# Pooled attention and a four-expert mixture: keys and values loaded as two accumulating halves, and weight combinations moved

## The chip, the cores and the metric

The kernel runs on one core of one Trainium2 chip. A core has five engines that run side by side, each through its own list of instructions in order: TensorE (PE, matrix products), VectorE (DVE), ScalarE (ACT), GpSimd (POOL) and SyncE (SP). POOL and SP here mostly start transfers (DMAs), which 16 DMA engines carry out. Engines wait for each other and for transfers through semaphores. The metric is the device time of one execution in microseconds (us); lower is better. The program before takes 526.44 us (median of three runs, 525.48 to 526.85). The profiled execution took 525.31 us, and its profile spans 523.6 us, at a granted TensorE clock of 0.998.

## The reference

Two computations follow each other. First, attention with pooled keys and values, for 8 batches, 8 heads, 576 positions and 64 columns: each group of eight consecutive positions of k and v is averaged to 72 positions, and every query attends to these.

```
k_p = k.reshape(B, H, 72, 8, D).mean(axis=3)      # v_p likewise
scores = q @ k_p^T / sqrt(D)
attn = exp(scores - max);  attn = attn / sum(attn)
x = attn @ v_p
```

Then a mixture of four experts on the 4608 rows of x (512 columns), with normalised probabilities p:

```
out = sum over e of  p[:, e] * ( relu(x @ w1[e]) @ w2[e] )     # w1: 512x1024, w2: 1024x512
```

## The kernel before, in words

**Order of the work.** The rows are taken in nine chunks c of 512: chunks 0 to 7 are the first 512 positions of each batch, chunk 8 collects the 64 remaining positions of all batches. For each chunk there are four steps, one per expert e. In a step, PE makes the expert's first product (the functions up_plain, up_half and up_seven, or up_down, which also makes the step before's second product), and down makes the second product of the step before. The attention of batch b = c + 1 is woven into chunk c, so that its x is ready when chunk b begins.

**Seven products instead of eight.** up_seven and up_down multiply 2x2 blocks with seven block products instead of eight. This needs sums and differences of blocks: of the weights w1 (combine_w1(e), four operations of 128x1024 each, L586 to L589), of w2 for experts 1 and 2 (combine_w2, L626 to L629), of x (forms_of, L602) and of the hidden values (sums_of, L701 to L704). They run on DVE, except combine_w2 of expert 2 and combine_w1 of expert 0, which are given to POOL. Expert 0 uses plain products (up_half, up_plain) in chunks 0 and 1 and the seven products from chunk 2 on; expert 1 uses plain products in chunk 0 alone. S3 overwrites the block A21, so it may only be formed once the plain products with that block are done.

**How the order is written.** The order on each engine is written out by hand. The code counts points: each step has 16, reached by point() and slot(). A plan maps a point to small functions (the plans of second_attention and attention(c); in the latter the entry n stands for point 2n + 1 of the chunk, so n runs from 0 to 31). slot() also takes the next function from the list forms_due, which holds the combinations. An entry `lambda: None` in that list, called nothing, delays the rest by one slot. Such a position sets the order in which an engine gets its instructions, and which earlier ones it must wait for; an engine whose inputs are ready does not wait for PE to reach the point.

**Keys and values.** load_kv fetches one batch's k or v on POOL's queue as 72 partitions x 8 heads x 8 positions x 64 columns, turned from float32 to bf16 on the way. DVE then adds the eight positions in three halvings: first adds 4 to 4 (L205, 72x1024), rest adds 2 to 2 (L210, 72x512) and 1 to 1 into the pooled tile (L213; twice for keys, into kp, and once for values, into vps). All this is done for two halves of the heads. All k, and v of batches 3 to 7, use one buffer, raw; v of batches 1 and 2 use the space of w2_t, which later holds the combined w2. Because there is one buffer, the values of a batch can only be fetched when its keys are folded, and the next keys when the values are folded.

**Around it.** keys(b) transposes the pooled keys by a transfer of SP (kp to kpT, L227), queries(b) the queries (L245), turn the finished x (L406). loads_wait is a one-element copy on POOL that waits for kpT (L234), and so holds POOL's later loads back until that transpose has landed. scores (L262, exponent at L266), context (L385, then reciprocal and division on DVE, L366 and L367) are the attention proper. On DVE there are further the relu sums of the seven products (L686), which free the PSUM banks that PE writes next, and the additions into the output rows (L761, L831).

Of the kernel before, what the change touches and what calls it, by code (L numbers as in the profile page):

```python
# [11 lines left out]
ALU = mybir.AluOpType  # L12
AX = mybir.AxisListType
BF16 = mybir.dt.bfloat16
# [4 lines left out]
def kernel(  # L19
# [55 lines left out]
    w2_t = wpool.tile([P, len(SPLIT), 3, FCH // 2, TH], BF16, name="w2_t")  # L75
    h_s = wpool.tile([P, 3, FCH // 2, TH], BF16, name="h_s")

    raws = {}
    q_rems = {}

# [1 line left out]
    halves = [slice(i * H // 2, (i + 1) * H // 2) for i in range(2)]  # L82

    def load_kv(b, src, nm):
        if b in (1, 2) and nm == "vraw":
            raw = w2_t[0:SP].rearrange("p a b f d -> p (a b f d)")[:, 0:H * POOL * D].rearrange(
                "p (h r d) -> p h r d", h=H, r=POOL
            )
        else:
            raw = rawpool.tile([SP, H, POOL, D], BF16, name="raw")[:]  # L90
        nc.gpsimd.dma_start(
            out=raw, in_=src[b].rearrange("h (j r) d -> j h r d", r=POOL)
        )
        raws[(nm, b)] = raw

    def load_first(src, nm, hs):
        if nm not in raws:
# [34 lines left out]
    def load_k(b):  # L132
        load_kv(b, k, "kraw")

    def load_v(b):
        load_kv(b, v, "vraw")
# [64 lines left out]
    def fold_parts(nm, b, hs, last):  # L201

        def first():
            raw = raws[(nm, b)]
            nc.vector.tensor_add(out=raw[:, hs, 0:4, :], in0=raw[:, hs, 0:4, :],  # L205
                                 in1=raw[:, hs, 4:8, :])

        def rest():
            raw = raws[(nm, b)]
            nc.vector.tensor_add(out=raw[:, hs, 0:2, :], in0=raw[:, hs, 0:2, :],  # L210
                                 in1=raw[:, hs, 2:4, :])
            for out in last(hs):
                nc.vector.tensor_add(out=out, in0=raw[:, hs, 0, :], in1=raw[:, hs, 1, :])  # L213

        return [first, rest]

    def key_parts(b):
        return [part for hs in halves for part in fold_parts(
            "kraw", b, hs, lambda hs: [kp[0:SP, hs, dup, :] for dup in range(2)])]
# [13 lines left out]
    def loads_wait(b):  # L233
        nc.gpsimd.tensor_copy(out=mark[:], in_=state[("kpT", b)][0:1, 0, 0:1])  # L234
# [268 lines left out]
    def second_attention():  # L503

        lo, hi = halves

        return {
            42: [lambda: fold_keys(1, lo)],
            44: [lambda: fold_keys(1, hi), lambda: load_k(2)],
            47: [second_keys],  # L510
            50: [lambda: second_queries(0)],
            51: [lambda: second_queries(1), lambda: load_q(2), lambda: load_q_rem(2)],
            53: [lambda: scores(1, 0)],
            55: [lambda: scores(1, 1)],
            56: [lambda: fold_values(1, lo)],
            57: [lambda: scores(1, 2)],
            58: [lambda: fold_values(1, hi)],
            59: [lambda: scores(1, 3)],
            60: [lambda: context(1, 0), lambda: turn(1, 0)],
            61: [lambda: context(1, 1), lambda: turn(1, 1)],  # L520
            62: [lambda: context(1, 2), lambda: turn(1, 2)],
            63: [lambda: context(1, 3), lambda: turn(1, 3)],
            66: [lambda: load_v(2)],
        }

    def attention(c):

        lo, hi = halves
        b = c + 1
        plan = {}  # L530

        def add(n, *what):
            plan.setdefault(n, []).extend(what)

        if c % 2:
            i = c // 2
            add(18, lambda: rem_queries(i))
            add(23, lambda: rem_scores(i))
            add(26, lambda: rem_context(i))
            add(27, lambda: rem_turn(i))  # L540
        if b == B:
            for part in forms_of(B):
                add(31, part)
            return plan
        if c == 1:
            keyed = 1
            add(0, lambda: queries(b))
            for n, part in enumerate(key_parts(b)):
                add(n // 2, part)
        else:  # L550
            keyed = 1
            for n, part in enumerate(key_parts(b)[2:]):
                add(n, part)
        scored, valued, mixed = 7, 8 if c > 1 else 6, 11
        add(keyed, lambda: keys(b), lambda: loads_wait(b))
        if c > 1:
            add(keyed + 1, lambda: load_v(b))
        if b + 1 < B:
            add(keyed + 1, lambda: (load_q(b + 1), load_q_rem(b + 1)))
        for pair in range(NPAIR):  # L560
            add(scored + pair, lambda pair=pair: scores(b, pair))
        for n, part in enumerate(value_parts(b)):
            add(valued + n, part)
        if b + 1 < B:
            add(valued + 4, lambda: queries(b + 1), lambda: load_k(b + 1))
            for n, part in enumerate(key_parts(b + 1)[:2]):
                add(30 + n, part)
        for r in range(NR):
            add(mixed + r, lambda r=r: context(b, r))
            add(mixed + 1 + r, lambda r=r: turn(b, r))  # L570
        for n, part in enumerate(forms_of(b)):
            add((20, 21, 28, 29)[n], part)
        return plan
# [274 lines left out]
    with tc.manual_schedule(engines={ENG.PE, ENG.DVE, ENG.Activation, ENG.Pool, ENG.SP}):  # L848
# [52 lines left out]
        for s in range(len(steps) + 1):  # L901
# [84 lines left out]
```

The softmax here doesn't subtract the row's maximum and nothing guards it: scores larger than these inputs give would overflow.

## Time and profile before

| what | value |
|---|---|
| median time | 526.44 us |
| span of the profile | 523.6 us |
| PE busy | 504.0 us (96%) |
| DVE busy | 355.4 us (68%) |
| ACT busy | 267.5 us (51%) |
| POOL busy | 67.5 us (13%) |
| POOL's loads (queue q0) | 33744 packets, 31.0% of 16 DMA engines |
| k and v loads, whole batches | 14 of 576 KB each |

A busy row gives the time in which an engine had an instruction running, with its share of the span and the number of instructions. In the second part of the page the span is cut into 40 slices of 13.1 us, and a digit is the busy share in tenths. A line of the timeline gives start, duration, engine, line of the code, operation, output and inputs by tile name, shapes and number; the brackets at its end give the idle time before it and what ended that. In a table of stages the columns are the stretch, its length, then for PE, its weight loads, DVE, ACT and POOL the busy us and the number of instructions, the granted clock, the busy share of the DMA engines and their GB/s.

### The profile page before, as it was taken

How to read it: one execution, taken by the hardware profiler on the slowest of the kernel's cores; microseconds unless marked ns; L12 is line 12 of the kernel's file. 1: busy time of each engine (PE TensorE's matmuls, PEld its weight loads, DVE VectorE, ACT ScalarE, POOL GpSimd, SP SyncE). 2: the span in 40 equal slices, each digit the busy share in tenths (PEclk: the TensorE clock that was granted, in tenths of full speed). 3: DMA queues.
4: the chain of work that ended last, by engine and by line, in shares of the span. 5: the costliest groups of instructions: out<-in, count | busy, mean ns of one | idle time of the engine just before them, and what ended most of it. 6: DMA issues, size and time to landing. Idle time of an engine off the chain costs nothing.

```text
span 523.6 us, 10155 instructions
## 1 busy us (share of the span) xinstructions
PE 504.0 (96%) x4171; PEld 363.5 (69%) x4171; DVE 355.4 (68%) x649; ACT 267.5 (51%) x467; POOL 67.5 (13%) x80
## 2 busy tenths in 40 slices
PE   8898989969999999999999999999999999999996
PEld 4745644558757876688668866886588768866883
DVE  2434787897857884878677876787677546764674
ACT  3653434636465545565465546653655446544650
POOL 8362102860020002000100020000000000000000
PEclk9999999999999999999999999999999999999999
DMA  9999999510199207920696059403510110011003
GB/s 133 207 206 206 199 149 179 107 30 1 24 169 107 25 0 142 145 36 11 106 143 65 2 94 157 70 11 57 94 32 0 41 52 1 11 42 40 1 1 80
DMA packets 75133, 41.56 MB, mean 79 GB/s; under 512 B 44480, under 2 KB 70464, under 8 KB 75088
## 3 DMA queue, kind: packets, MB, share of 16 engines
q0 software_dynamic: 33744, 22.63, 31.0%
q1 hardware_dynamic: 41344, 18.29, 18.7%
q8 instruction: 32, 0.52, 0.4%
q14 instruction: 13, 0.11, 0.1%
HBM read 45.16 MB, written 9.44 MB: 104 GB/s over the span
## 4 chain that ended last, share of the span: by engine, by line
PE 71%; DVE 13%; DMA 10%; POOL 2%; issue 2%; ACT 1%; POOLq 0%; ACTq 0%; SPq 0%; DVEq 0%
PE g_ps L638 30%; PE o_ps L817 19%; PE u_ps L755 16%; DMA w_bf<-in_moe_w_dram 5%; DMA raw<-in_v_dram 3%; DVE H_sb L686 3%; DVE acc L761 3%; DMA kpT<-kp 2%; PE h_ps L656 1%; PE two L262 1%; PE two L385 1%; POOL w_bf L142 1%; DVE h_s L701 1%; DVE x_tok L367 1%; DVE H_sb L702 1%
## 5 line engine op out<-in xcount | busy, mean ns | idle before, releaser
L638 PEld LDWEIGHTS <-w_bf 128*128 128x128 bf16 x1848 | 176.1, 98 | 49.5 <-issue 10.7
L817 PE MATMUL o_ps<-w_bf,H_sb 128*128 128x512 bf16 x640 | 161.5, 379 | 0.2 <-DMA w_bf<-in_moe_w_dram 0.2
L682 ACT COPY r<-g_ps 128x512 f32<-128x512 f32 x166 | 97.4, 586 | 106.3 <-PE g_ps L638 102.4
L638 PE MATMUL g_ps<-xf,w_bf 128*128 128x256 bf16 x1056 | 148.4, 272 | 2.8 <-DVE H_sb L686 1.8
L686 DVE CUSTOM_DVE_ANT_0 H_sb<-g_ps,r 128x512 bf16<-128x512 f32 x166 | 113.9, 687 | 48.1 <-ACT r L682 33.3
L761 DVE SCALAR_TENSOR_TENSOR acc<-u_ps,p_all,acc 128x512 f32<-128x512 f32 (+1 forms) x128 | 78.0, 612 | 43.8 <-ACT u_ps L781 43.1
L638 PE MATMUL g_ps<-xT,w_bf 128*128 128x256 bf16 x696 | 99.9, 273 | 2.0 <-DVE H_sb L686 2.0
L817 PEld LDWEIGHTS <-H_sb 128*128 128x128 bf16 x640 | 62.5, 98 | 46.1 <-issue 0.4
L689 ACT ACTIVATE H_sb<-g_ps 128x512 bf16<-128x512 f32 x98 | 58.4, 596 | 29.7 <-PE g_ps L638 29.7
L755 PEld LDWEIGHTS <-H_sb 128*128 128x128 bf16 x512 | 49.4, 98 | 8.2 <-DVE H_sb L702 2.4
L755 PE MATMUL u_ps<-w_bf,H_sb 128*128 128x256 bf16 x384 | 52.4, 273 | 1.1 <-DVE H_sb L702 0.9
L755 PEld LDWEIGHTS <-h_s 128*128 128x128 bf16 x384 | 37.5, 98 | 6.1 <-DVE h_s L703 1.8
L831 DVE SCALAR_TENSOR_TENSOR acc<-o_ps,p_all,acc 128x512 f32<-128x512 f32 x44 | 32.7, 746 | 11.3 <-PE o_ps L817 11.3
L755 PE MATMUL u_ps<-w_t,h_s 128*128 128x256 bf16 x256 | 38.4, 273 | 1.5 <-DVE h_s L703 1.5
L266 ACT ACTIVATE expT<-two 72x1024 bf16<-72x1024 f32 x28 | 28.6, 1020 | 13.4 <-PE two L262 13.4
L767 ACT COPY g_ps<-g_ps 128x512 f32<-128x512 f32 x32 | 18.3, 572 | 27.9 <-PE g_ps L638 27.9
L828 ACT ACTIVATE acc<-o_ps,p_all 128x512 f32<-128x512 f32 x36 | 24.8, 690 | 7.0 <-PE o_ps L817 7.0
L234 POOL COPY mark<-kpT 1x1 bf16<-1x1 bf16 x6 | 1.3, 218 | 205.9 <-DMA kpT<-kp 205.9
L781 ACT COPY u_ps<-u_ps 128x256 f32<-128x256 f32 x32 | 11.4, 357 | 26.7 <-PE u_ps L755 26.7
L205 DVE TENSOR_TENSOR raw<-raw 72x1024 bf16<-72x1024 bf16 x22 | 15.0, 681 | 13.5 <-DMA raw<-in_v_dram 13.5
L367 DVE TENSOR_TENSOR x_tok<-two,inv 128x512 bf16<-128x512 f32 x32 | 22.1, 691 | 1.1
L385 PEld LDWEIGHTS <-expT 72*128 72x128 bf16 x256 | 12.0, 98 | 12.4 <-DVE x_tok L367 4.8
(113 smaller groups left out, 377.2 us busy)
## 6 DMA issues: line engine op xcount, KB each, us to landing
out_dram<-acc SPq DMA_DIRECT2D x32, 256.0 KB, 2.9
w_bf<-in_moe_w_dram POOLq DMA_DIRECT2D x16, 256.0 KB, 9.7
w_bf<-in_moe_w_dram POOLq DMA_DIRECT2D x4, 1024.0 KB, 16.9
raw<-in_k_dram POOLq DMA_DIRECT2D x7, 576.0 KB, 11.4
q_sb<-in_q_dram POOLq DMA_DIRECT2D x7, 512.0 KB, 11.9
raw<-in_v_dram POOLq DMA_DIRECT2D x5, 576.0 KB, 8.1
w_t<-in_v_dram POOLq DMA_DIRECT2D x2, 576.0 KB, 13.2
out_dram<-acc SPq DMA_DIRECT2D x8, 128.0 KB, 2.3
```

Of the source, the lines that this page charges most:

```text
L266: nc.scalar.activation(out=state[("expT", b)][:, 2 * pair:2 * pair + 2].rearrange("j h r s p -> j s (h r) p"), in_=two[0:SP].rearrange("j ...
L367: nc.vector.tensor_tensor(out=x_tok[:], in0=c_ps[:, :, :, 0:D], in1=inv[:].unsqueeze(3).to_broadcast([P, 2, NPAIR, D]), op=ALU.mult,)
L638: nc.tensor.matmul(bank[:, t, :], lhsT=w1_bf[:, e, block, kc, lo:lo + P], rhs=x[:, kc, :], start=(first and t == 0 and kc == 0), stop=(t = ...
L682: nc.scalar.copy(out=r[:], in_=ps[:])
L686: nc.vector._custom_dve(TENSOR_ADD_SAT, out=out, in0=ps[:], in1=r[:], s0=BIG, s1=0.0)
L689: nc.scalar.activation(out=out, in_=ps[:], func=ACT.Relu)
L755: nc.tensor.matmul(out, lhsT=lhs[0][:, lhs[1] + f, lhs[2]], rhs=rhs[0][:, rhs[1] + f, rhs[2]], start=(start and f == 0), stop=(f == FCH // ...
L761: nc.vector.scalar_tensor_tensor(out=acc, in0=ps, scalar=prob, in1=acc, op0=ALU.mult, op1=ALU.add,)
L767: nc.scalar.copy(out=s[:], in_=g[:])
L817: nc.tensor.matmul(sums[r][:], lhsT=hidden[(c, e)][:, fc, r * P:(r + 1) * P], rhs=w2_bf[:, e, fc, :], start=(fc == 0), stop=(fc == FCH - 1),)
L828: nc.scalar.activation(out=accs[(c, r)][:], in_=o_ps[:], func=ACT.Copy, scale=prob)
L831: nc.vector.scalar_tensor_tensor(out=dst, in0=o_ps[:], scalar=prob, in1=dst, op0=ALU.mult, op1=ALU.add,)
```

## The change

Three things are changed.

For batches 3 to 7, k and v arrive as two transfers each: load_half(…, 0) writes positions 0 to 3 of each group into one of two half-size places of the new tile raw_kv, and load_half(…, 1) adds positions 4 to 7 to them in flight. The first halving on DVE (first) is thereby left out for these batches, and k and v of a batch have a place each. Batches 1 and 2 keep plain loads: k into the whole of raw_kv, v into w2_t.

The loads move. Both first halves of batch b + 1 are listed at n = 17 of chunk b - 1, the queries of batch b + 2 and both second halves at n = 19; loads_wait stays for batch 2 alone. The pooled value parts of a batch stand at n = 9 and 10 (before: 8 to 11).

The combinations move. combine_w1(0) goes from POOL to DVE: two operations at the start of step s = 4, the third at its end, the fourth at the start of s = 5. combine_w1(3) begins four slots later. combine_w2 of expert 2 stays on POOL, with a fixed point.

```diff
+    raw_kv = rawpool.tile([SP, 2, H, POOL // 2, D], BF16, name="raw_kv")
...
     def load_kv(b, src, nm):
-        if b in (1, 2) and nm == "vraw":
-            raw = w2_t[0:SP].rearrange("p a b f d -> p (a b f d)")[:, 0:H * POOL * D].rearrange(
-                "p (h r d) -> p h r d", h=H, r=POOL
-            )
-        else:
-            raw = rawpool.tile([SP, H, POOL, D], BF16, name="raw")[:]
+        wide = (w2_t[0:SP].rearrange("p a b f d -> p (a b f d)")[:, 0:H * POOL * D] if nm == "vraw"
+                else raw_kv[:].rearrange("p a h r d -> p (a h r d)"))
+        raws[(nm, b)] = wide.rearrange("p (h r d) -> p h r d", h=H, r=POOL)
...
+    def load_half(b, src, nm, half):
+        raws[(nm, b)] = raw_kv[:, 0 if nm == "kraw" else 1]
+        lo = half * POOL // 2
+        nc.gpsimd.dma_start(
+            out=raws[(nm, b)],
+            in_=src[b].rearrange("h (j r) d -> j h r d", r=POOL)[:, :, lo:lo + POOL // 2],
+            accum_op=ALU.add if half else ALU.bypass,
+        )
+
+    def load_later(b, half):
+        load_half(b, k, "kraw", half)
+        load_half(b, v, "vraw", half)
...
-        return [first, rest]
+        return [first, rest] if b == 2 else [rest]
...
-            66: [lambda: load_v(2)],
+            64: [lambda: load_v(2)],
...
         if c == 1:
-            keyed = 1
-            add(0, lambda: queries(b))
-            for n, part in enumerate(key_parts(b)):
-                add(n // 2, part)
+            add(0, lambda: queries(b), *key_parts(b)[:2])
+            add(1, *key_parts(b)[2:])
+            add(1, lambda: keys(b), lambda: loads_wait(b))
+            add(1, lambda: (load_q(b + 1), load_q_rem(b + 1)))
         else:
-            keyed = 1
-            for n, part in enumerate(key_parts(b)[2:]):
-                add(n, part)
-        scored, valued, mixed = 7, 8 if c > 1 else 6, 11
-        add(keyed, lambda: keys(b), lambda: loads_wait(b))
-        if c > 1:
-            add(keyed + 1, lambda: load_v(b))
-        if b + 1 < B:
-            add(keyed + 1, lambda: (load_q(b + 1), load_q_rem(b + 1)))
+            add(0, key_parts(b)[1], lambda: keys(b))
+        scored, valued, mixed = 7, 9 if c > 1 else 6, 11
...
         if b + 1 < B:
-            add(valued + 4, lambda: queries(b + 1), lambda: load_k(b + 1))
-            for n, part in enumerate(key_parts(b + 1)[:2]):
-                add(30 + n, part)
+            add(12, lambda: queries(b + 1))
+            add(17, lambda: load_later(b + 1, 0))
+            if b + 2 < B:
+                add(19, lambda: (load_q(b + 2), load_q_rem(b + 2)))
+            add(19, lambda: load_later(b + 1, 1))
+            add(30, key_parts(b + 1)[0])
...
             elif s == 2:
-                forms_due.extend(combine_w1(3))
+                forms_due.extend(nothing + combine_w1(3))
             elif s == 4:
-                forms_due.extend(nothing[:2] + combine_w1(1) + combine_x(1))
+                w, x = combine_w1(0), combine_x(1)
+                forms_due.extend(w[:2] + combine_w1(1) + x[:1] + [lambda: (x[1](), w[2]())])
             elif s == 5:
-                forms_due.extend(nothing[:3] + combine_w2(SPLIT[0]))
-                forms_due.extend(combine_w2(SPLIT[1], nc.gpsimd) + combine_w1(0, nc.gpsimd))
+                forms_due.extend(w[3:] + nothing[:2] + combine_w2(SPLIT[0]))
+                placed.setdefault(at + 5, []).extend(combine_w2(SPLIT[1], nc.gpsimd))
```

More of the change, by code (lines that the diff above doesn't have):

```diff
@@ L84, in load_kv @@
     def load_kv(b, src, nm):
-        if b in (1, 2) and nm == "vraw":
-            raw = w2_t[0:SP].rearrange("p a b f d -> p (a b f d)")[:, 0:H * POOL * D].rearrange(
-                "p (h r d) -> p h r d", h=H, r=POOL
-            )
-        else:
-            raw = rawpool.tile([SP, H, POOL, D], BF16, name="raw")[:]
+        wide = (w2_t[0:SP].rearrange("p a b f d -> p (a b f d)")[:, 0:H * POOL * D] if nm == "vraw"
+                else raw_kv[:].rearrange("p a h r d -> p (a h r d)"))
+        raws[(nm, b)] = wide.rearrange("p (h r d) -> p h r d", h=H, r=POOL)
         nc.gpsimd.dma_start(
-            out=raw, in_=src[b].rearrange("h (j r) d -> j h r d", r=POOL)
+            out=raws[(nm, b)], in_=src[b].rearrange("h (j r) d -> j h r d", r=POOL)
         )
-        raws[(nm, b)] = raw
+    def load_half(b, src, nm, half):
[9 more added lines that the diff above has]
+        load_half(b, v, "vraw", half)
     def load_first(src, nm, hs):
```

## The prediction

> **What bounds the kernel now.** I read the page's busy row and slices first, then the busy time of each engine by stage, then the timeline of each engine around the stages where TensorE (PE) loses time, and the chain of waits for what ends them.
>
> ```profile
> PE 504.0 (96%) x4171; PEld 363.5 (69%) x4171; DVE 355.4 (68%) x649; ACT 267.5 (51%) x467; POOL 67.5 (13%) x80
> ...
> PE   8898989969999999999999999999999999999996
> ```
>
> PE is busy 96% of a 523.6 us span and its row is a wall of nines after the tenth slice (13.1 us each). Whatever the change takes off another engine is worth nothing unless PE waits for it there. The stages (span, then busy us of each engine) say where PE waits:
>
> ```profile
> 40.10:56.30 16.20, 13.37 (x94) 8.55 (x93) 10.04 (x20) 5.20 (x9) 3.12 (x4) 1.00 1.28 203
> ...
> 107.00:120.00 13.00, 8.85 (x79) 7.30 (x77) 11.32 (x13) 4.92 (x11) 6.13 (x3) 1.00 0.10 20
> 141.80:195.50 53.70, 53.62 (x450) 40.38 (x449) 40.03 (x75) 29.64 (x52) 3.49 (x5) 1.00 0.59 76
> ```
>
> The whole of batch 3's attention stage (the third row) has 0.08 us of idle PE. The 16.2 us before 56.3 have 2.8, and the 13 us after 107 have 4.15. PE's timeline names the releasers:
>
> ```profile
> 48.67 1.03 PE L638 MATMUL g_ps<-xT,w_bf 128*128 128x256 bf16 x8 [1.99 <-DVE H_sb L686]
> ...
> 109.36 1.03 PE L638 MATMUL g_ps<-xf,w_bf 128*128 128x256 bf16 x8 [1.77 <-DVE H_sb L686]
> 111.29 1.05 PE L755 MATMUL u_ps<-w_bf,H_sb 128*128 128x256 bf16 x8 [0.90 <-DVE H_sb L702]
> 113.82 0.61 PE L755 MATMUL u_ps<-w_t,h_s 128*128 128x256 bf16 x4 [1.48 <-DVE h_s L703]
> ...
> 212.63 0.29 PE L385 MATMUL two<-vp,expT 72*128 72x65 bf16 x4 [0.83 <-DVE vp L213]
> ```
>
> Each time it is VectorE (DVE). Why DVE was late, by its own and GpSimd's (POOL) timeline:
>
> ```profile
> 46.13 0.69 DVE L586 TENSOR_TENSOR w_bf<-w_bf 128x1024 bf16<-128x1024 bf16 x1 [7.51 <-DMA w_bf<-in_moe_w_dram]
> ...
> 106.94 1.77 DVE L701 TENSOR_TENSOR h_s<-H_sb 128x1024 bf16<-128x1024 bf16 x1
> 109.23 2.00 DVE L702 TENSOR_TENSOR H_sb<-H_sb 128x1024 bf16<-128x1024 bf16 x1
> 111.16 2.60 DVE L703 TENSOR_TENSOR h_s<-h_s,H_sb 128x1024 bf16<-128x1024 bf16 x1
> 113.79 0.69 DVE L704 TENSOR_TENSOR h_s<-H_sb,h_s 128x1024 bf16<-128x1024 bf16 x1
> ```
> ```profile
> 103.06 2.57 POOL L586 TENSOR_TENSOR w_bf<-w_bf 128x1024 bf16<-128x1024 bf16 x1
> 105.71 2.45 POOL L587 TENSOR_TENSOR w_bf<-w_bf 128x1024 bf16<-128x1024 bf16 x1
> 108.24 2.45 POOL L588 TENSOR_TENSOR w_bf<-w_bf 128x1024 bf16<-128x1024 bf16 x1
> 110.65 2.56 POOL L589 TENSOR_TENSOR w_bf<-w_bf 128x1024 bf16<-128x1024 bf16 x1
> ```
>
> At 46.13 DVE had stood 7.51 us in front of a w1 load of expert 3, with the relu sum that PE needed queued behind it. From 107 to 113.8 the same 128x1024 operation takes 1.77 to 2.60 us while POOL runs combine_w1(0), and 0.69 us at 113.79, after POOL ended at 113.2. For the value wait at 212.63:
>
> ```profile
> 208.66 0.69 DVE L205 TENSOR_TENSOR raw<-raw 72x1024 bf16<-72x1024 bf16 x1 [3.67 <-DMA raw<-in_v_dram]
> ```
>
> [...]
>
> **The change, part by part.**
> (1) combine_w1(0) leaves POOL for DVE. POOL's four combine_w2(2) operations still start when batch 2's values are folded (93.70) and end at 103.06; now nothing follows. So L701 to L703 lose their company: 0.69 us each instead of 1.77, 2.00, 2.60, and L629 at 105.01 loses about 0.5 of its 1.17. Replaying DVE in order: L629 ends at 105.6, reciprocal and divide at 106.45, L701 at 107.1, the relu sum at 107.7, L702 at 108.4, L703 at 109.1. PE needs the relu sum at 107.43 (0.3 lost), then has 8 matmuls (0.87) and 8 more (0.87), and reaches at 109.5 what it started at 113.82. **Gain 4.3 us.** The price is four 0.69 us additions on DVE, two at the start of the step at 76 us, two near 89 to 92. DVE idles 0.48, 1.31 and 1.57 us at 84.6, 88.0 and 92.3, while PE runs up_plain, whose relus are ScalarE's: hidden. The key transpose moves from 80.3 to 81.7, scores use it at 87.9: hidden. The waits for x_tok at 99 to 105 (1.1 us) stay, since combine_w2(1) on DVE still meets POOL. Ends: 3.0 if the backlog of 96 to 105 carries over, 4.8 if it vanishes.
>
> (2) combine_w1(3) starts four slots later, near 46.6 instead of being reached at 38.6; the load landed at 46.03. The wait of 7.51 goes, and with it the 2.16 us from PE's due time (46.51) to 48.67. But batch 1's key folds follow at once: from 46.6 DVE has two 0.68 additions, two 0.60 relu sums and two folds of 1.57, with gaps for PE, and ends the second fold near 53.6. PE wants it (second_keys) near 52.5, so a stall of about 1.1 replaces the 0.83 there now, and batch 1's queries, landing at 56.78, cost up to 0.5. **Gain 1.8 us** (1.2 to 2.3).
>
> (3) Values of batches 3 to 7 come before the previous batch ends instead of after the key transpose (the mark copy of L234 held their issue: 200.37 for batch 4). The value waits of PE, 1.00 us at 212.63 and 0.49 at 376.19 by start-to-start times, go. **Gain 1.4 us** (1.0 to 1.6).
>
> (4) Four first folds (72x1024, 681 ns) leave DVE for each of five batches: 20 x 0.681 = 13.6 us, against 4 x 0.69 = 2.8 added. As those stages have at most some tenths of idle PE, nearly all of it lies beside PE's work. **Gain 0.3 us** (0 to 1.0).
>
> (5) The accumulating transfers. POOL runs ahead of PE, so the slot numbers set only the order: the first key half goes when its buffer is free (keys folded, slot 0), the value half after the value folds (slot 10, near 158 in batch 3's stage), then the query load after the query transpose (near 165), then the two accumulations, some 7 us of queue later, near 172. Plain cost of a half: its packets have the queries' form, 512 bytes each; those take 60 to 68 ns in the trace. 576 x 68 ns / 16 engines = 2.4 us, the low end. For the accumulating half no row exists; I take twice to three times that, 5 to 7 us[...], and work out what would hurt. Keys are folded at slot 30, which ran at 190.2: 18 us of room. Values are folded at slot 9 of the next stage, near 208.7, behind both accumulations: 36 us for two, 18 each. So up to 18 us a piece (500 ns a packet, seven times plain) is hidden. Behind POOL's new wait for a half to land stand only the other accumulation and the next batch's loads, none of them needed within 18 us. Ten more issues at 0.84 us are 8.4 us of POOL, under PE. **Cost 0**, high end open. The removed mark lets the transposes and loads overlap as they do now at 158 to 174; a DVE wait for xT of 1.15 us at 174.3 may grow by 1 or 2 us, PE feeling some tenths.
>
> Sum: 4.3 + 1.8 + 1.4 + 0.3 = 7.8 us; 526.4 - 7.8 = **518.6 us**.
>
> **Rivals.**
> A, accumulation becomes the wait: 21 us each. Keys at 193, 3 us late, values at 214, 5 us later than now. The value wait of 1.0 us at 212.63 followed a landing at 208.56, so PE loses 5 to 6 us in each of five batches: 518.6 + 27 = 546 us. For it: no row of the trace prices the operation. Against: it takes seven times a plain packet. Chance 0.08.
> B, DVE itself is the bound around 107, since the four additions come back on it: the backlog of 96 to 105 and the 2.8 us eat most of part 1, 1.5 us instead of 4.3: 521.4 us. For: DVE is busy 9.9 of 10 us from 100 to 110. Against: 3.4 us of idle DVE before 92.3. Chance 0.17.
> C, gains given back: part 2's time reappears as DMA waits before 75 us (the DMA engines are full until 73) and part 1's in the next stage: within 1.5 us of before, 525.5 us. Chance 0.05.
> D, fewer folds also shorten the small waits that the releasers hide, 1 us in each of three stages: 515.6 us. Chance 0.10.
> The forecast keeps 0.60.
>
> **How the numbers follow.** Forecast terms from end to end give 3.0 + 1.2 + 1.0 + 0 = 5.2, or 4.8 + 2.3 + 1.6 + 1.0 = 9.7: 516.7 to 521.2. Taking in B, and most of D, and 0.9 for small losses of part 5, the range is 516.0 to 522.6; A, C and the rest of D stay outside, below 0.2. Faster by over 0.3% is below 524.9: forecast, B, D, 0.87. Within 0.3%: 0.05. Slower: 0.08.
>
> **What would show it.** Part 1: POOL ends its combinations near 101, L701 to L704 take 0.69 us, and PE's three waits at their start shrink to under half a microsecond; DVE shows four more combine additions before 92. Part 2: no wait of L586 on the w1 load over 1 us, PE's wait for H_sb near 48 gone, one for kp near 1 us. Part 3: no PE wait for vp. Part 4: the 72x1024 group falls from 22 to 2, DVE busy near 340. Part 5: accumulating key halves land before 188 in the third stage and DVE has no wait on raw. The prediction is wrong if DVE waits for raw at slot 30, if L701 still meets a POOL operation, or if the stage from 41 to 75 stalls on loads.

## The result, and the profile after

The changed kernel takes 518.94 us (median of four runs, 517.8 to 519.35) against 526.5 us for the kernel before in the same comparison (four runs, 525.48 to 526.85). The ratio is 0.9856, with a 95% interval of 0.9835 to 0.9877: faster by 7.6 us. The profile's span falls from 523.6 to 517.1 us. Of the executions below, one of 22 with the later combine_w1(3) alone took 585.66 us at a mean clock of 0.852, and ratios and mean clocks leave it out.

The page's busy row and slices, after:

```profile
PE 501.0 (97%) x4125; PEld 363.0 (70%) x4171; DVE 341.3 (66%) x633; ACT 267.3 (52%) x467; POOL 71.1 (14%) x81
...
PE   8899889999999999999999999999999999999996
```

The rows hardly look different. The 14.1 us that DVE lost are nearly twice what the kernel gained, so the busy shares don't say where the time came from. (PE's busy time is 3.0 us less although its work is the same: 46 of its 4171 matmul records are missing in this trace.) The stages of the prediction after the change; the second is cut down to the seven microseconds in which the waits lay:

```profile
40.10:54.60 14.50, 13.43 (x97) 8.92 (x97) 9.64 (x19) 5.45 (x10) 3.45 (x5) 1.00 1.28 204
...
105.00:112.00 7.00, 6.81 (x64) 5.96 (x62) 6.02 (x12) 3.99 (x8) 0.00 (x0) 1.00 1.76 128
141.00:194.00 53.00, 52.72 (x442) 39.96 (x445) 36.99 (x70) 29.18 (x52) 6.14 (x6) 1.00 0.54 74
```

The first stage has 1.07 us of idle PE instead of 2.8. In the second, POOL computes nothing any more, and PE has 0.19 us idle in seven. The third was full before and is full now: DVE has 3 us less to do there, and PE idles for 0.28 us. PE's timeline at the places where it waited:

```profile
54.01 0.30 PE L319 MATMUL kpt_ps<-ident,kp 72*128 72x72 bf16 x4 [1.02 <-DVE kp L208]
57.18 0.62 PE L329 MATMUL qt_ps<-ident,q_sb 128*128 128x128 bf16 x8 [0.47 <-DMA q_sb<-in_q_dram]
...
106.28 1.03 PE L644 MATMUL g_ps<-xf,w_bf 128*128 128x256 bf16 x8 [0.19 <-DVE H_sb L692]
...
108.03 0.60 PE L761 MATMUL u_ps<-w_t,h_s 128*128 128x256 bf16 x4
116.88 0.60 PE L761 MATMUL u_ps<-w_t,H_sb 128*128 128x256 bf16 x4 [0.39 <-DVE acc L767]
206.42 0.42 PE L395 MATMUL two<-vp,expT 72*128 72x65 bf16 x8
```

L644 and L761 are L638 and L755 of before. Near 48 us no wait is left; its price is the wait of 1.02 us for kp at 54.01 and that of 0.47 us for the queries at 57.18. The waits of 1.77, 0.90 and 1.48 us around 111 have become one of 0.19 us, and the value wait at 206.42 is gone. One wait is new: 0.39 us at 116.88. DVE's timeline says why:

```profile
47.65 0.68 DVE L592 TENSOR_TENSOR w_bf<-w_bf 128x1024 bf16<-128x1024 bf16 x1
...
104.95 0.68 DVE L707 TENSOR_TENSOR h_s<-H_sb 128x1024 bf16<-128x1024 bf16 x1
106.15 0.68 DVE L708 TENSOR_TENSOR H_sb<-H_sb 128x1024 bf16<-128x1024 bf16 x1
106.75 0.68 DVE L709 TENSOR_TENSOR h_s<-h_s,H_sb 128x1024 bf16<-128x1024 bf16 x1
...
115.74 0.43 DVE L608 TENSOR_TENSOR xf<-xT 128x512 bf16<-128x512 bf16 x1 [3.10 <-DMA xT<-x_tok]
```

L592 (L586 of before) no longer waits for the weights. L707 to L709 (L701 to L703) take 0.68 us instead of 1.77, 2.00 and 2.60. At 115.74 DVE stands 3.10 us for the transposed x, which shares the DMA engines with the loads that the change put there (the last of it lands 10.6 us after its issue, and 2.4 us after it with these loads held, below). POOL's timeline:

```profile
99.03 2.58 POOL L635 TENSOR_TENSOR w_t<-w_bf,w_t 128x1024 bf16<-128x1024 bf16 x1
101.55 0.86 POOL L96 DMA_DIRECT2D raw_kv<-in_k_dram  x1
...
160.32 1.46 POOL L96 DMA_DIRECT2D raw_kv<-in_k_dram  x1
161.19 2.04 POOL L96 DMA_DIRECT2D raw_kv<-in_v_dram  x1
```

POOL's last combination ends at 101.6; directly behind it the first halves of batch 3 are issued. The last two lines are the accumulating halves of batch 4: the record of the second begins while the first is still running, and the two together keep POOL busy from 160.32 to 163.23, some 1.46 us each. A plain half at 101.55 takes 0.86.

**Where the time came from, instruction by instruction.** PE's order was not changed: the n-th of its 4171 weight loads is the same one in both traces. The difference of their start times is what has been gained up to there. The fourth column is the same difference for a second profile of the unaltered changed kernel, taken later (the run at the end of the experiments):

```
start     start    gained   gained in the    what lies in between
before    after    so far   second profile
 48.67    46.19     2.49        2.31         the w1(3) wait is gone
 56.13    54.01     2.12        2.42         wait for kp longer (first profile)
 58.56    57.17     1.39        2.05         new wait for the queries (first profile)
 79.84    78.35     1.49        1.57         new wait for the transposed x (second profile)
113.83   108.03     5.80        5.88         combine_w1(0) no longer on POOL
122.56   117.48     5.08        5.88         DVE late for xT (first profile)
212.63   206.55     6.08        6.88         value wait of batch 4 gone
376.19   369.62     6.56        7.36         value wait of batch 7 gone
   end      end     6.57        7.36
```

The path explains 6.57 us in one profile and 7.36 in the other. The medians differ by 7.56 us in the first comparison and by 6.59 in the one that goes with the second profile. So differences of a microsecond between two single profiles are within their spread; the section on the clock has what averages add to this.

### The profile page after: what moved, and what is told of

The parts are those of the page before. It is cut to its first block, busy times and chain, and to the rows that moved or that the text cites. A ratio compares the mean times of both kernels' runs of the same rounds, so it can differ in the third digit from the quotient of the medians.

```text
span 517.1 us, 10085 instructions
## 1 busy us (share of the span) xinstructions
PE 501.0 (97%) x4125; PEld 363.0 (70%) x4171; DVE 341.3 (66%) x633; ACT 267.3 (52%) x467; POOL 71.1 (14%) x81
## 3 DMA queue, kind: packets, MB, share of 16 engines
q0 software_dynamic: 41584, 22.65, 35.8%
## 4 chain that ended last, share of the span: by engine, by line
PE 76%; DMA 10%; DVE 7%; POOL 2%; issue 2%; ACT 1%; POOLq 0%; ACTq 0%; DVEq 0%
PE g_ps L644 33%; PE o_ps L823 22%; PE u_ps L761 16%; DMA w_bf<-in_moe_w_dram 4%; DMA q_sb<-in_q_dram 4%; DMA xT<-x_tok 2%; DVE acc L767 2%; PE two L272 2%; DVE H_sb L692 1%; PE h_ps L662 1%; PE two L395 1%; POOL w_bf L152 1%; DVE x_tok L377 1%; DVE h_s L707 1%; DVE xf L608 1%
## 5 line engine op out<-in xcount | busy, mean ns | idle before, releaser
L644 PEld LDWEIGHTS <-w_bf 128*128 128x128 bf16 x1848 | 176.0, 98 | 46.1 <-issue 7.0
L823 PE MATMUL o_ps<-w_bf,H_sb 128*128 128x512 bf16 x598 | 154.1, 379 | 2.2
L644 PE MATMUL g_ps<-xf,w_bf 128*128 128x256 bf16 x1056 | 148.5, 273 | 1.2 <-ACT g_ps L773 0.7
L644 PE MATMUL g_ps<-xT,w_bf 128*128 128x256 bf16 x696 | 99.9, 273 | 0.0
L761 PEld LDWEIGHTS <-H_sb 128*128 128x128 bf16 x512 | 49.4, 98 | 7.7 <-DVE H_sb L708 1.3
L761 PE MATMUL u_ps<-w_bf,H_sb 128*128 128x256 bf16 x384 | 52.4, 273 | 0.2
L761 PEld LDWEIGHTS <-h_s 128*128 128x128 bf16 x384 | 37.5, 98 | 4.4
L761 PE MATMUL u_ps<-w_t,h_s 128*128 128x256 bf16 x256 | 38.4, 273 | 0.0
L96 POOL DMA_DIRECT2D raw_kv<-in_v_dram x10 | 13.6, 1360 | 73.3 <-DVE vp L223 65.8
L96 POOL DMA_DIRECT2D raw_kv<-in_k_dram x10 | 11.5, 1150 | 84.8 <-DVE kp L223 84.8
L761 PE MATMUL u_ps<-w_t,H_sb 128*128 128x256 bf16 x128 | 19.3, 273 | 0.4 <-DVE acc L767 0.4
```

Source lines behind the costliest of these rows:

```text
L96: nc.gpsimd.dma_start(out=raws[(nm, b)], in_=src[b].rearrange("h (j r) d -> j h r d", r=POOL)[:, :, lo:lo + POOL // 2], accum_op=ALU.add i ...
L644: nc.tensor.matmul(bank[:, t, :], lhsT=w1_bf[:, e, block, kc, lo:lo + P], rhs=x[:, kc, :], start=(first and t == 0 and kc == 0), stop=(t = ...
L761: nc.tensor.matmul(out, lhsT=lhs[0][:, lhs[1] + f, lhs[2]], rhs=rhs[0][:, rhs[1] + f, rhs[2]], start=(start and f == 0), stop=(f == FCH // ...
L823: nc.tensor.matmul(sums[r][:], lhsT=hidden[(c, e)][:, fc, r * P:(r + 1) * P], rhs=w2_bf[:, e, fc, :], start=(fc == 0), stop=(fc == FCH - 1),)
```

## The experiments

**Theory:** the gain is PE's waits that go, some 4.4 us of it by taking POOL's reads away from DVE's additions, 1.4 by the later combine_w1(3) and 1.3 by the earlier values; the accumulations and the missing folds change nothing. **Rivals:** the relief of DVE (20 folds) brings the time; or the transfers do; or POOL's being busy at all, not its reads, slows DVE. In the edits, `nothing` is a list of four empty entries, each of which delays what follows by a slot. Times are medians, and each ratio is to the kernel before.

**Before, with combine_w1(0) on DVE alone.**

```diff
             elif s == 4:
-                forms_due.extend(nothing[:2] + combine_w1(1) + combine_x(1))
+                w, x = combine_w1(0), combine_x(1)
+                forms_due.extend(w[:2] + combine_w1(1) + x[:1] + [lambda: (x[1](), w[2]())])
             elif s == 5:
-                forms_due.extend(nothing[:3] + combine_w2(SPLIT[0]))
-                forms_due.extend(combine_w2(SPLIT[1], nc.gpsimd) + combine_w1(0, nc.gpsimd))
+                forms_due.extend(w[3:] + nothing[:2] + combine_w2(SPLIT[0]))
+                placed.setdefault(at + 5, []).extend(combine_w2(SPLIT[1], nc.gpsimd))
```

> The kernel before with one part of the change: combine_w1(0) on VectorE instead of GpSimd, at the places the change gives it. Theory[...]: L701 to L703 fall from 1.77, 2.00 and 2.60 us to 0.69, PE's three waits at 109 to 114 shrink to some 0.3 us together, 4.4 us less than before: ratio near 0.9915. Rival (VectorE has no room for the four extra additions): at most 1.5 us less, ratio 0.997 or more, with PE waits for VectorE between 76 and 107 that are not there before.

Measured: 520.33 us, ratio 0.990 (0.9875 to 0.9924). In the trace 4.51 us are gained by the weight load of 113.83, 4.30 of it at the three waits near 110, as in the change (4.31). At the end it is 4.99: the value wait of batch 7 (0.48 us) is absent here too, although the loads are those of before. This one part is worth 4.3 us in the path and some 5 in the time, with plain loads and all folds in place; the rival that the transfers or the folds bring most of the time is out.

**Before, with the later combine_w1(3) alone.**

```diff
-                forms_due.extend(combine_w1(3))
+                forms_due.extend(nothing + combine_w1(3))
```

> The kernel before with one part of the change: combine_w1(3) four slots later. Theory: the wait of L586 on the w1 load and PE's 2 us behind it go, a longer wait for kp and a wait for batch 1's queries take part of it back, 1.4 us stay: ratio near 0.9973. Rival (the stage is bound by its loads, and the time returns as other load waits before 75 us): under 0.5 us, ratio 0.999 or more.

Measured: 525.56 us, ratio 0.9993 (0.9979 to 1.0007). The expected ratio of 0.9973 lies outside: a miss. The trace has the gain, 2.30 us at 46.38 and still 1.44 at 112.4, and loses it between 110.0 and 116.9. The table of stages there (after the busy times come the granted clock, the DMA share and GB/s):

```profile
105.00:110.00 5.00, 2.33 (x21) 1.70 (x19) 5.00 (x5) 2.00 (x4) 4.92 (x3) 1.00 0.27 53
110.00:115.00 5.00, 4.22 (x21) 2.71 (x20) 3.84 (x4) 0.94 (x2) 1.77 (x1) 0.50 0.00 0
```

From 105 to 110 PE is busy for 2.33 of 5 us, in the stall that this kernel keeps. Then its clock stands at half for 6.83 us: four matmuls of L638 take 1.06 us at 113.20, and 0.60 us at 117.18, when it is full again. So the term of 1.4 us is real in the path and was not seen in the time of this kernel alone; no run shows it in the time.

**The change without the moved combinations** (transfers, and the plan that goes with them, alone).

```diff
-                forms_due.extend(nothing + combine_w1(3))
+                forms_due.extend(combine_w1(3))
             elif s == 4:
-                w, x = combine_w1(0), combine_x(1)
-                forms_due.extend(w[:2] + combine_w1(1) + x[:1] + [lambda: (x[1](), w[2]())])
+                forms_due.extend(nothing[:2] + combine_w1(1) + combine_x(1))
             elif s == 5:
-                forms_due.extend(w[3:] + nothing[:2] + combine_w2(SPLIT[0]))
-                placed.setdefault(at + 5, []).extend(combine_w2(SPLIT[1], nc.gpsimd))
+                forms_due.extend(nothing[:3] + combine_w2(SPLIT[0]))
+                forms_due.extend(combine_w2(SPLIT[1], nc.gpsimd) + combine_w1(0, nc.gpsimd))
```

> The changed kernel with the combinations in the order and on the engines of before, so that only the two accumulating transfers and the moved loads remain. Theory (their worth is the two value waits of PE, 0.8 and 0.5 us, less what a clash of loads and transposes in chunk 1 costs): 0.6 to 1.3 us less than before, ratio 0.9975 to 0.999. Rival (20 folds less on VectorE, 13.6 us of its work, are the gain): 3 us or more less, ratio 0.994 or below.

Measured: 524.5 us, ratio 0.9975 (0.9961 to 0.9988): about 1.3 us, as the theory has it, and the rival's 3 us are out. Its profile is only 0.24 us ahead at the end: the two value waits are gone (0.99 and 0.48 us), but the clock stands at half for 3.41 us, and POOL's last three operations of combine_w1(0), now behind the loads, meet DVE again near 120. The stall near 107 only took another shape. The timeline of this kernel:

```profile
102.19 2.13 POOL L635 TENSOR_TENSOR w_t<-w_bf,w_t 128x1024 bf16<-128x1024 bf16 x1
...
102.46 4.49 DVE L634 TENSOR_TENSOR w_bf<-w_bf 128x1024 bf16<-128x1024 bf16 x1
...
104.28 2.12 POOL L592 TENSOR_TENSOR w_bf<-w_bf 128x1024 bf16<-128x1024 bf16 x1
```

One DVE addition met two of POOL's that followed each other directly, and lasted for 4.49 us, until 0.55 us after both had ended (106.95 against 106.40); PE then waited 3.46 us for x_tok behind it.

**The change, with POOL reading again in the critical stretch.** Four POOL subtractions that read w1 and write a tile that is not filled until later, behind combine_w2(2): a stand-in for combine_w1(0) that changes nothing in the results.

```diff
+                placed.setdefault(at + 5, []).extend([lambda: nc.gpsimd.tensor_sub(
+                    out=x_rem[:, 0:2], in0=w1_bf[:, 0, A11], in1=w1_bf[:, 0, A12])] * 4)
```

> The changed kernel plus four more GpSimd subtractions of 128x1024 right behind combine_w2(2), which read two blocks of w1 and write a place that is overwritten later (they are extra work; VectorE keeps combine_w1(0)). Theory (GpSimd's reads slow VectorE): L707 to L709 rise from 0.68 us to about 1.8, 2.0 and 2.6, PE's waits at 105 to 112 come back with some 4.4 us, time 522.5 to 524, and TensorE's granted clock may dip there as in the two kernels that kept this stall. Rival (it was VectorE's own share of work, or GpSimd's being late with its loads): no more than 1 us over the changed kernel's 518.9.

**The change, with POOL writing there instead.**

```diff
+                placed.setdefault(at + 5, []).extend([lambda: nc.gpsimd.memset(x_rem[:, 0:2], 0.0)] * 10)
```

> The changed kernel plus ten GpSimd memsets of 128x1024 at the same place: GpSimd is as busy there, but reads nothing. Theory: VectorE's additions stay at 0.68 us and the time within 0.2% of the changed kernel's 518.9. Rival (a busy GpSimd is enough): L707 to L709 slow down as with reads, 522 us or more.

Measured: with reads 524.53 us, ratio 0.9972 (0.9958 to 0.9985); with writes 518.23 us, ratio 0.9863 (0.9841 to 0.9885), the time of the change itself. The timeline with reads, then with writes:

```profile
101.09 10.15 POOL L935 TENSOR_TENSOR x_rem<-w_bf 128x1024 bf16<-128x1024 bf16 x4
...
107.27 2.00 DVE L708 TENSOR_TENSOR H_sb<-H_sb 128x1024 bf16<-128x1024 bf16 x1
109.19 2.60 DVE L709 TENSOR_TENSOR h_s<-h_s,H_sb 128x1024 bf16<-128x1024 bf16 x1
```
```profile
101.72 10.02 POOL L935 MEMSET x_rem<- 128x1024 bf16 x10
...
106.93 0.68 DVE L709 TENSOR_TENSOR h_s<-h_s,H_sb 128x1024 bf16<-128x1024 bf16 x1
```

In both POOL is busy for 10 us beside the same DVE additions, and in both its loads of batch 3 are issued 10 us later (at 111.19 and 111.69 instead of 101.55). With reads the additions take 2.00 and 2.60 us, to the hundredth what they took before the change, and the path, 0.5 us ahead of the changed kernel's when the stall begins, is 3.9 us behind at 111.85 (5.6 after a stretch of half clock). The time is half a microsecond above the 522.5 to 524 expected. With writes the additions take 0.68 us. POOL's reads cost the time, not its being busy and not its late loads.

**The change without the accumulating transfers.** The pooled keys and values of batches 3 to 7 are then sums of four positions only.

```diff
-            add(19, lambda: load_later(b + 1, 1))
```

> The changed kernel without the ten second (accumulating) transfers; the pooled keys and values of batches 3 to 7 are then sums of four positions only. Theory (the accumulation is wholly hidden): within 0.2% of the changed kernel, ratio to before 0.985 to 0.987. Rival (the accumulation or GpSimd's wait for it costs PE time): 1 us or more faster than the changed kernel, ratio 0.983 or below.

Measured: 518.94 us, ratio 0.9861 (0.9836 to 0.9887), the change's own median. Ten accumulating transfers cost nothing that can be measured.

**The change in quarters.** A plain transfer and three accumulating ones of two positions each, and 20 folds of 72x512 fewer.

```diff
-        lo = half * POOL // 2
+        lo = half * 2
-            out=raws[(nm, b)],
-            in_=src[b].rearrange("h (j r) d -> j h r d", r=POOL)[:, :, lo:lo + POOL // 2],
+            out=raws[(nm, b)][:, :, 0:2],
+            in_=src[b].rearrange("h (j r) d -> j h r d", r=POOL)[:, :, lo:lo + 2],
...
-            nc.vector.tensor_add(out=raw[:, hs, 0:2, :], in0=raw[:, hs, 0:2, :],
-                                 in1=raw[:, hs, 2:4, :])
+            if b == 2:
+                nc.vector.tensor_add(out=raw[:, hs, 0:2, :], in0=raw[:, hs, 0:2, :],
+                                     in1=raw[:, hs, 2:4, :])
...
-            add(19, lambda: load_later(b + 1, 1))
+            for part in (1, 2, 3):
+                add(19, lambda part=part: load_later(b + 1, part))
```

> The changed kernel with keys and values of batches 3 to 7 in four transfers each, one plain and three accumulating, of two positions: three chained additions on the DMA engines instead of one, and 20 folds of 72x512 less on VectorE. Theory (there is ample room behind the loads, and VectorE's relief is worth nothing): within 0.3% of the changed kernel, 518 to 520, with the last key part landed before slot 30. Rival (accumulation becomes the wait): VectorE waits for the keys or values, 521 or more.

Measured: 518.45 us, ratio 0.9854 (0.9828 to 0.9881): the time is that of the change. But a chain of three accumulations is not wholly hidden. In the chunk in which it starts latest it passes its limit, as DVE's timeline and PE's behind it show:

```profile
133.00 0.49 DVE L224 TENSOR_TENSOR kp<-raw_kv 72x256 bf16<-72x256 bf16 x2 [2.27 <-DMA raw_kv<-in_k_dram]
```
```profile
134.53 1.03 PE L646 MATMUL g_ps<-xf,w_bf 128*128 128x256 bf16 x8 [0.44 <-DVE H_sb L694]
```

The last key part landed at 132.97, where it had been expected ahead of this slot: a miss. DVE stood 2.27 us for it, the relu sum behind it came late, and PE lost 0.60 us against the second profile of the changed kernel, which has no wait there. It is the only one of the five batches with such a wait. With a single accumulation the same keys land at 125.11 and are first read at 131.43, so 6.3 us are left.

**The change with 20 folds given back to DVE**, as a maximum of a tile with itself, which leaves its values as they are.

```diff
+            if b != 2:
+                nc.vector.tensor_tensor(out=raw[:, hs], in0=raw[:, hs], in1=raw[:, hs], op=ALU.max)
```

> The changed kernel with the removed VectorE work put back: ahead of each remaining fold of batches 3 to 7 an in-place maximum of the 72x1024 half with itself, which leaves the values as they are (20 instructions, 13.6 us of VectorE). Theory (VectorE's relief is beside PE's work): 0 to 0.5 us over the changed kernel, 518.9 to 519.4. Rival (the relief is part of the gain): 2 us or more over it, 521 or above.

Measured: 518.9 us, ratio 0.987 (0.9849 to 0.9892). They are 13.6 us of DVE, 679 ns each. The third stage:

```profile
141.00:194.00 53.00, 52.71 (x443) 39.91 (x445) 39.55 (x75) 29.27 (x52) 6.14 (x6) 1.00 0.57 76
```

DVE has 39.55 us to do instead of 36.99, and PE is busy for 52.71 instead of 52.72 us. From the weight load of 122.56 on, behind which all 20 folds lie, the path gains the same 1.48 us as the changed kernel's. (Ahead of them this execution lost 1.3 us near 79 to a wait for the transposed x, and was spared the loss at 116.88.) The relief of DVE is worth nothing in this kernel. What the halves also give is room: keys and values of a batch have a place each in the space of the former single buffer, which the earlier value loads use. Whether the values could come earlier without accumulation was not tried.

**The change with batch 3's first halves held** until the transposed x of chunk 1 has landed, by a one-element copy on POOL. This is aimed at the new wait at 115.74.

```diff
+            if c == 1:
+                add(17, lambda: nc.gpsimd.tensor_copy(
+                    out=mark[:], in_=state[("xT", b)][0:1, 0, NT - 1:NT]))
             add(17, lambda: load_later(b + 1, 0))
```

> The changed kernel with one wait more: in chunk 1 a one-element GpSimd copy of the last column of the transposed x stands ahead of the first halves of batch 3, so that these loads start only when the transposes of x have landed. Theory (the changed kernel loses 0.65 us of PE at 116 to 118, where VectorE waits 3.1 us for a transpose that shares the DMA engines with these loads and the query load): that wait goes, 0.5 to 0.7 us less than the changed kernel, near 518.3. Rival (the loads are then late for slot 30 of chunk 1, or the wait moves elsewhere): same or slower.

Measured: 518.11 us, ratio 0.9861 (0.9838 to 0.9885). The path gains 0.64 us by the weight load of 116.9. That looked like proof until the changed kernel, unaltered, was profiled a second time (below). The hold does help the transposes: the last two of chunk 1's x land 2.4 us after their issue instead of 10.2 and 10.6.

**Two versions that should be faster still.** Both keep that hold and move combine_w2(2) from POOL to DVE as well, so that DVE meets no reads of POOL there; the second starts it two slots later.

```diff
-                forms_due.extend(w[3:] + nothing[:2] + combine_w2(SPLIT[0]))
-                placed.setdefault(at + 5, []).extend(combine_w2(SPLIT[1], nc.gpsimd))
+                forms_due.extend(w[3:] + nothing[:1] + combine_w2(SPLIT[0]) + combine_w2(SPLIT[1]))
```

> The changed kernel with the wait ahead of batch 3's first halves, and with combine_w2(2) on VectorE too, right behind combine_w2(1): GpSimd then computes nothing. Theory (the three PE waits for x_tok at 98 to 103, 1.1 us together, come from VectorE meeting GpSimd's combine_w2(2), which costs 2.56 and 1.18 us instead of 0.68): they go, about 0.6 to 1.1 us below the kernel with the wait alone (518.1), near 517.3. Rival (VectorE has no room for four more additions in the next step): no gain or slower, 518.1 or more.

```diff
+                forms_due.extend(w[3:] + nothing[:1] + combine_w2(SPLIT[0]) + nothing[:2]
+                                 + combine_w2(SPLIT[1]))
```

> As the kernel with all combinations on VectorE and the wait in chunk 1, but combine_w2(2) starts two slots later, behind the sums of the hidden values. Theory (there, the 1.16 us won at the x_tok waits were half lost again since two additions stood ahead of the relu sum that PE needs at 105.8): the 0.86 us stall at 105.8 falls to about 0.35 and the time is 0.5 us under that kernel's 517.97, near 517.4. Rival (the next step then has a late w2 or too much on VectorE): same or slower.

Measured: 517.97 us, ratio 0.9846 (0.9817 to 0.9875), for the first; 517.88 us (516.88 to 518.64), ratio 0.9861 (0.9832 to 0.9889), for the second. Neither reaches the 517.3 and 517.4 that were expected. In the first the x_tok waits go (1.16 us against the version with the hold alone), but DVE is late once more, and a stall of PE of 0.69 us at 105.75 (0.19 with the hold alone) takes more than half of it back. In the second that stall is gone, and half a microsecond shows up a little later, in PE's timeline:

```profile
111.25 0.92 PE L647 MATMUL g_ps<-xf,w_bf 128*128 128x256 bf16 x7 [0.49 <-DVE H_sb L695]
```

**The changed kernel again**, beside the last version.

> The changed kernel itself, beside the version above on the same chip: 518.5 to 519.3 expected; if the version above is better, it lies at least 1 us below this one.

Measured: 518.45 us (517.93 to 518.69), ratio 0.9867 (0.9842 to 0.9892). The last version's path is 1.07 us shorter in the profile, the medians differ by 0.57 us, and the runs overlap: the microsecond expected of it is not there, and a better version is not established. This second profile also corrects the reading of the held loads. DVE's timeline:

```profile
113.65 0.43 DVE L608 TENSOR_TENSOR xf<-xT 128x512 bf16<-128x512 bf16 x1 [1.09 <-DMA xT<-x_tok]
```

Without any hold the wait for xT is 1.09 instead of 3.10 us here, PE's loss of 0.72 us is absent, and the span is 516.2 us. Among the profiles without the stall near 107, DVE waits for xT in all five in which batch 3's first halves are issued at 101 to 104 (0.75 to 3.10 us), and in none of the four in which they come later; so the loads do delay the transposes. But PE lost time by it in one of the five only, and what the hold brings was not shown. Another wait differs as much. In PE's timeline of this second profile:

```profile
78.27 1.89 PE L662 MATMUL h_ps<-xT,w_bf 128*128 128x512 bf16 x8 [0.30 <-DMA xT<-x_tok]
```

The first profile and that of before have no such wait, the later combine_w1(3) alone has one of 0.22 us, and the kernel with folds given back one of 1.02.

## Why the prediction was right

**Step 1, combine_w1(0) off POOL: right.** Forecast 4.3 us, measured 4.31 in both profiles of the change (from 79.84 to 113.83) and 4.30 alone. The reads of POOL are shown as the cause by the pair of reads and writes (2.00 and 2.60 us with reads, 0.68 with writes). The x_tok waits stayed, as said; putting combine_w2(2) on DVE removes them.

**Step 2, combine_w1(3) later: right in kind and within its range.** Forecast 1.8 us (1.2 to 2.3), measured 1.49 and 1.57 by the weight load of 79.84. The wait of 2.16 us went as worked out (2.15 to 2.16 in both). What it costs differs between executions: the stall for kp was 1.02 us in the first profile (1.1 forecast) and 0.56 in the second, the queries cost the full half microsecond in the first, and the second paid for the transposed x near 78 instead. That last price was not in this step; it is rival C on a small scale. The step shows in the path alone, not in a time.

**Step 3, values earlier: right in the path.** Forecast 1.4 us, measured 1.00 + 0.48 = 1.48. The 1.00 us of batch 4 is gained in all profiles with the moved loads and in neither kernel that keeps the loads of before. The 0.48 of batch 7 was gained by combine_w1(0) on DVE alone as well, so it isn't shown to be due to the loads.

**Step 4, fewer folds: 0 instead of 0.3.** With them given back, the time is the same.

**Step 5, accumulations hidden: right, with the price oversized and the tightest place overlooked.** "Twice to three times" the 2.4 us of a plain half had been taken, 5 to 7 us: an estimate of the author's, as the trace of before has no accumulating transfer. In chunk 1, where the two run together, 1152 packets of 512 bytes take 93 ns each: 1152 x 93 / 16 engines = 6.7 us for both, 3.3 each. Queueing counts for more than that. After an issue at 160.32 the key half of batch 4 lands at 170.38, 10.1 us later, and the value half, issued at 161.19, at 173.50, because the queries are ahead of them (issued at 158.74, landed at 165.68). Their first folds stand at 185.07 and 201.88, so 14.7 and 28.4 us are left (the room had been worked out from 190 and 208.7). The prediction took this one stage for all. In chunk 1 POOL is busy with combine_w2(2) and then waits, so the same accumulations are issued at 117.3, and 6.3 us are left for the keys; the version in quarters used that up. The page's rows for the value halves and the queue:

```profile
q0 software_dynamic: 41584, 22.65, 35.8%
...
raw_kv<-in_v_dram POOLq DMA_DIRECT2D x10, 288.0 KB, 9.3
```

The price shows as the queue's share, 35.8% against 31.0%, for the same bytes: it has 7840 packets more. The wait of POOL for a first half was an assumption of the prediction. The trace shows it once, 7.5 us ahead of the issue at 324.20 (values of batch 7; the other nine first halves had landed when POOL came to the second), and it does no harm: the half issued there lands at 332.41 and is first read at 364.96. What was not foreseen is the wait in chunk 1: POOL stood 12.5 us for the transposed last queries. It did no harm either. The loss for xT had been priced at "some tenths" of PE; it was 0.72 us in one profile and absent in the other.

**The sum was right partly by luck.** The path's terms add up to 4.31 + 1.49 + 1.48 + 0 - 0.72 = 6.56 us in the first profile and to 4.31 + 1.57 + 1.48 = 7.36 in the second, not to 7.8. The clock, a term that the prediction didn't have, goes with about a microsecond of the mean gain (below). The 95% interval of the measured ratio spans 6.5 to 8.7 us, so that 518.6 fell within 0.4 us of 518.94 is more than the working could promise.

**Rivals.** The accumulation is no wait; DVE is no bound near 107 (6.0 of 7 us busy, PE 0.19 idle); the gains were given back only in part, by waits for transposed x near 78 and 117 that came and went between executions; and the extra relief is not there.

## What to carry to other kernels

Price a change by the waits of the engine that sets the end, instruction against instruction, and not by busy time: here DVE had 14 us less to do, the gain had nothing to do with that, and giving 13.6 of them back changed nothing. When you look for the room of a transfer, look in the stage where it is issued latest. If a DVE addition takes two to four times its usual time (here 1.77 to 2.60 us instead of 0.68), look for GpSimd reading beside it before you look for too much work. Once gains get down to a microsecond, profile the unaltered kernel twice before you explain one of its waits.

## What the hardware showed that was not expected

**The kernels that keep the stall ran at a lower clock.** The kernels that keep the stall near 107 sometimes run on at half the TensorE clock during it or behind it: for 6.83 us from 110.0 in the one with the later combine_w1(3) alone, for 3.41 us from 108.6 in the one with the transfers alone, for 6.83 us from 108.7 in the one with POOL's reads. The profiles of the changed kernel, of combine_w1(0) on DVE, and of the versions with folds back, quarters, writes or held loads have no such stretch while PE works; the one without accumulations has one of 3.41 us, at 18.5 us, in another stage. The mean granted clock over the runs says the same (for before, of two of four sets of them; the other two have 0.9944 and 0.9963, and the four versions not listed 0.9978 to 0.9988):

```
kernel                              near 107      mean clock (runs)
before                              stall         0.9945 (41), 0.9952 (27)
combine_w1(3) later alone           stall         0.9928 (21)
transfers alone                     stall         0.9957 (20)
change with POOL's reads            stall         0.9940 (22)
change                              no stall      0.9978 (4)
combine_w1(0) on DVE alone          no stall      0.9983 (6)
change without accumulations        no stall      0.9980 (5)
change with folds back              no stall      0.9982 (6)
change with POOL's writes           no stall      0.9982 (5)
```

Over all four sets, the 31 of 90 runs of before with a mean clock of at least 0.998 have a mean span of 523.02 us, the other 59 one of 524.74. All 90 have 524.15, and the ten runs of the changed kernel 516.85. So of a mean gain of 7.3 us, 6.2 remain if before is taken at the full clock alone, and 1.1 go with the clock. Adding POOL's reads to the changed kernel brought the stall and the lower clock together (0.9940).

The lengths of these stretches are 3.41 and 6.83 us. In the 3.41 us before each of the four PE was idle for 2.20 us (later combine_w1(3)), 2.69 (transfers, where a single gap of 3.46 us ends at 107.85), 2.04 (POOL's reads) and 1.32 (without accumulations, at 18.5). The profile of before has 3.41 us with 2.38 idle, and no stretch. So the idle time just before does not decide alone in these traces. What does, and why the later combine_w1(3) alone has the lowest clock of all, stays open.

**What accumulating costs a transfer.** DVE's group of 72x1024 folds falls from 22 to 2, and no engine has instructions in their place: the additions lie in the transfers. In chunk 1 of the changed kernel packets of 512 bytes take 93 ns in the two accumulating halves, against 71 ns in the plain key half issued at 135.18, which runs beside no other load, and 90 ns in plain halves and queries that run beside transposes (103 to 116 us). How much of the 93 is the addition and how much the company was not separated. An accumulating issue keeps POOL busy for 1.4 to 1.5 us, a plain one for 0.8 to 0.9.

**How far a read of POOL stretches DVE.** From 0.68 us to 1.77, 2.00 and 2.60 next to POOL operations of about 2.5 us, and to 4.49 us beside two that followed directly. In these traces the stretch isn't a factor but what is left of POOL's operation: before the change the three additions end at 108.71, 111.23 and 113.76, POOL's L587 to L589 at 108.16, 110.69 and 113.21, so DVE ends 0.54 to 0.55 us after POOL each time, as it does behind the two (0.55). Ten memsets, 10.02 us of them, stretched nothing.
